# The leftover rows of w2: four loads of 32 rows made one load of 128 rows

## The chip, the cores and the metric

The kernel runs on one core of a Trainium2 chip. The metric is the device time of the whole program in microseconds, as the median of the runs of one kernel. The profile comes from one further execution, recorded by the hardware profiler. Its span, from the first to the last instruction, is a little shorter than the time of the same execution.

## The reference

The input x has 2048 rows of 640 elements in bf16. Two blocks are computed from it and mixed by a gate:

```python
x = A_x
g = _sigmoid((x * gate_w).sum(-1, keepdims=True))
a = _A_ref(x, A_wqkv, A_wo)                       # linear attention, 32 heads of 20
b = _B_ref(x, B_w1, B_w2, B_w3, B_w4)             # shift MLP, then an MLP with F = 1728
return g * a + (1 - g) * b
```

The part that the change touches is the middle of block B. There c is 160, and g0 to g3 are the four groups of c columns of h, shifted by 1, -1, 2 and -2 rows:

```python
h = _gelu(_layernorm(x, axis=-1) @ w1)
c = D // 4
...
hs = jnp.concatenate([g0, g1, g2, g3], axis=-1) @ w2
x1 = x + hs
h2 = _gelu(_layernorm(x1, axis=-1) @ w3) @ w4
return x1 + h2
```

## The kernel before, in words

A product over 640 columns is made in DC = 5 chunks of 128 rows of the weight, one chunk per matmul of an accumulation. The rows of x are worked on in 16 chunks of 128 (NCH) or in 4 tiles of 512 (NT).

The four groups of h that are shifted differently have 160 columns each (CG), which is not a multiple of 128. So the first 128 columns of group g make chunk g (g = 0 to 3), and the four leftovers of 32 columns share chunk 4: the leftover of group g lies in partitions 32g to 32g + 31. The activations in `hsT` and the rows of w2 in `w2_sb` are laid out in this way. `w2_sb[:, 4, :]` therefore holds rows 128 to 159, 288 to 319, 448 to 479 and 608 to 639 of w2.

All large loads are issued by SyncE (`sp`), in the order of the text: the first chunks of x and k's weights (some of these by ScalarE), x transposed by the DMA (L123), q's weights (L138), the rest of x (L120, called a second time), v's weights (L140), w1 (L141), six blocks of wo (L143), w2 (L144 to L148) and w3 (L149). w2's loads are one for the first two whole blocks (L144), then in a loop over g the strips of g = 0 and g = 1 (L148), the block of g = 2 (L147), its strip, the block of g = 3 and its strip. w4 is loaded much later (L602 to L604). A schedule written out by hand (`manual_schedule`) keeps the order of the text on every engine.

After w3, SyncE's queue holds the DMA transposes of the linear attention's matrix (L323, written from `gs`, which ScalarE evacuates at L321) and of the normalised rows of x (`lnx`, L311).

TensorE's order is: k (L187), q (L242), the sums over rows (L319), then for the first tile of rows the product with w1 (L353), the small products of the attention (L372, L257, L386), the product with w2 (`w2_unit`, L436, 5 chunks for each half of 320 columns), more of w1, then w3 (`w3_unit`, L486), interleaved with w2 for later tiles and with the attention's output (L467), and at last w4 (L525, L561). On GpSimd, L171 copies the leftover columns of w1 together once w1 has landed.

The few lines that matter here besides the diff:

```python
for hf in range(2):
    for fc in range(DC):
        nc.tensor.matmul(pt[:, hf, 0:HD], lhsT=hsT[:, fc, 2 + c * P:2 + (c + 1) * P],
                         rhs=w2_sb[:, fc, hf * HD:(hf + 1) * HD], start=(fc == 0), stop=(fc == DC - 1))
```

Of the kernel before, what the change touches and what calls it, by code (L numbers as in the profile page):

```python
# [16 lines left out]
def kernel(  # L17
# [14 lines left out]
    P = 128  # L32
# [12 lines left out]
    CG = D // 4  # L45
# [34 lines left out]
    w2_sb = const.tile([P, DC, D], BF16)  # L80
# [36 lines left out]
    sp, aq, gq = nc.sync, nc.scalar, nc.gpsimd  # L117
# [24 lines left out]
    for g in range(NG):  # L142
        sp.dma_start(wo_sb[:, g, :], A_wo[row0[g]:row0[g] + P, :])  # L143
    sp.dma_start(w2_sb[:, 0:2, :], B_w2[0:2 * CG, :].rearrange("(g p) f -> p g f", g=2)[0:P])  # L144
    for g in range(4):
        if g >= 2:
            sp.dma_start(w2_sb[:, g, :], B_w2[CG * g:CG * g + P, :])  # L147
        sp.dma_start(w2_sb[32 * g:32 * (g + 1), 4, :], B_w2[CG * g + P:CG * (g + 1), :])  # L148
    sp.dma_start(w3_sb[:], B_w3.rearrange("(c p) f -> p c f", p=P))  # L149


# [510 lines left out]
```

## Time and profile before

| What | Value |
|---|---|
| time, median of 3 runs | 263.35 us (263.07 to 265.75) |
| time of the profiled execution | 263.29 us |
| its span | 261.6 us |
| granted TensorE clock, mean | 0.998 |
| DMA packets, bytes | 57618, 28.28 MB |
| DVE, ACT, POOL busy | 141.3, 93.4, 28.0 us |
| first L436 (w2 is read) starts | 86.2 us |
| first L486 (w3 is read) starts | 102.4 us |

The times in a profile are microseconds from the start of the span. PE is TensorE, PEld its weight loads, DVE is VectorE, ACT is ScalarE, POOL is GpSimd; SPq is the queue of SyncE, which issues DMAs. `w_sb` stands for w1, w2, w3 and w4 alike, since the names are cut at the digits; the line tells them apart. The page's DMA row gives the mean busy share of the 16 DMA engines in 40 equal slices of the span, in tenths. The chain that ended last is followed back from the last instruction, at each step to what released it or to the instruction ahead of it on its engine.

### The profile page before, as it was taken

To read this page: it belongs to the slowest core of one execution; us is meant where nothing else is said; L and a number is where in the kernel's file an instruction comes from. 1 tells how busy PE (TensorE), PEld (TensorE's weight loads), DVE (VectorE), ACT (ScalarE), POOL (GpSimd) and SP (SyncE) were. 2 spreads that over 40 slices of the span, in tenths; PEclk is the share of its full clock that TensorE was granted. 3 is DMA by queue.
4 is the path that set the end of the run, shared out by engine and by line. 5 is a ranking of instruction groups with operands and counts; after the bars stand their busy time and mean duration, and the time that the engine had idled before them with its cause. 6 is when DMAs were issued, how large, how long until landed. Compare 5 with 4: busy or idle time off the path is not lost.

```text
span 261.6 us, 4116 instructions
## 1 busy us (share of the span) xinstructions
PE 255.6 (98%) x1601; PEld 151.4 (58%) x1625; DVE 141.3 (54%) x276; ACT 93.4 (36%) x144; POOL 28.0 (11%) x82
## 2 busy tenths in 40 slices
PE   7999999999999999999999999999999999999995
PEld 3777555688854644565464566455565555465553
DVE  2688778799947884866300398600287600125142
ACT  1555454321165446532343323342321443442100
POOL 3000040012220140131000131000122000000000
PEclk9999999999999999999999999999999999999999
DMA  7999996016675736997022124212123412211011
GB/s 200 201 185 370 364 287 267 0 28 123 123 103 77 213 71 139 173 315 95 7 43 40 20 53 95 75 23 60 20 53 70 102 20 43 65 34 64 0 50 53
DMA packets 57618, 28.28 MB, mean 108 GB/s; under 512 B 45566, under 2 KB 56830, under 8 KB 57598
## 3 DMA queue, kind: packets, MB, share of 16 engines
q1 hardware_dynamic: 57156, 27.52, 45.0%
q10 hardware_dynamic: 442, 0.49, 0.5%
q8 instruction: 13, 0.21, 0.3%
q14 instruction: 7, 0.06, 0.1%
HBM read 13.03 MB, written 3.60 MB: 64 GB/s over the span
## 4 chain that ended last, share of the span: by engine, by line
PE 96%; DMA 2%; issue 1%; SPq 0%; DVE 0%
PE pp L486 21%; PE pp L525 16%; PE pp L319 8%; PE pp L436 8%; PE pp L467 8%; PE pp L242 8%; PE pp L353 8%; PE pp L187 8%; PE pp L561 5%; DMA wk_sb<-in_A_wqkv_dram 2%; PE pp L496 1%; PE pp L517 1%; PE pp L386 1%; PE pp L372 1%; PE pp L257 0%
## 5 line engine op out<-in xcount | busy, mean ns | idle before, releaser
L486 PE MATMUL pp<-lnxT,w_sb 128*128 128x512 bf16 x249 | 59.8, 379 | 0.6
L488 ACT ACTIVATE h<-pp 128x1024 bf16<-128x1024 f32 (+1 forms) x28 | 26.9, 962 | 56.1 <-PE pp L486 56.1
L525 PE MATMUL pp<-h,w_sb 128*128 128x512 bf16 (+1 forms) x228 | 42.4, 343 | 0.3
L486 PEld LDWEIGHTS <-w_sb 128*128 128x128 bf16 x260 | 25.2, 98 | 26.9
L439 DVE TENSOR_TENSOR x<-pp,x_sb 128x640 f32<-128x640 f32 x16 | 13.1, 818 | 43.0 <-PE pp L436 42.9
L525 PEld LDWEIGHTS <-w_sb 128*128 128x128 bf16 x234 | 22.7, 98 | 19.5 <-issue 1.0
L179 ACT ACTIVATE e<-pp 128x640 bf16<-128x640 f32 (+1 forms) x26 | 21.5, 826 | 9.6 <-PE pp L242 9.6
L467 PE MATMUL pp<-m_sb,pqT 128*128 128x320 bf16 x160 | 24.3, 299 | 0.0
L473 DVE SCALAR_TENSOR_TENSOR x<-pp,gate,x 128x640 f32<-128x640 f32 x16 | 14.1, 883 | 18.3 <-PE pp L467 12.6
L436 PE MATMUL pp<-w_sb,hsT 128*128 128x320 bf16 x160 | 23.9, 299 | 0.0
L289 POOL TENSOR_SCALAR rstd<-mv 128x1 f32<-128x1 f32 (+1 forms) x20 | 7.7, 384 | 142.8 <-DVE mv L295 142.8
L187 PE MATMUL pp<-wk_sb,xT 128*128 128x320 bf16 (+1 forms) x160 | 22.5, 300 | 0.2
L319 PE MATMUL pp<-x_sb,pk 128*128 128x320 bf16 (+1 forms) x160 | 22.0, 300 | 0.0
L242 PE MATMUL pp<-xT,hsT 128*128 128x512 bf16 x98 | 21.6, 379 | 0.1
L319 PEld LDWEIGHTS <-pk 128*128 128x128 bf16 x160 | 18.8, 118 | 3.2
L436 PEld LDWEIGHTS <-hsT 128*128 128x128 bf16 x160 | 15.6, 98 | 8.0
L467 PEld LDWEIGHTS <-pqT 128*128 128x128 bf16 x160 | 15.7, 98 | 7.7
L538 DVE SCALAR_TENSOR_TENSOR oc<-pqT,omg,x 128x640 bf16<-128x640 bf16 x12 | 10.5, 877 | 16.8 <-DMA pqT<-hx 16.8
L187 PEld LDWEIGHTS <-xT 128*128 128x128 bf16 x160 | 15.5, 98 | 6.9 <-DVE xT L216 0.6
L353 PE MATMUL pp<-lnxT,w_sb 128*128 128x512 bf16 x77 | 17.9, 379 | 0.2
L242 PEld LDWEIGHTS <-hsT 128*128 128x128 bf16 x100 | 11.8, 118 | 9.7
L529 ACT CAST hx<-pp 128x512 bf16<-128x512 f32 x12 | 7.0, 585 | 22.5 <-PE pp L525 14.9
(80 smaller groups left out, 236.2 us busy)
## 6 DMA issues: line engine op xcount, KB each, us to landing
x_sb<-in_A_x_dram SPq DMA_DIRECT2D x1, 2240.0 KB
out_dram<-oc SPq DMA_DIRECT2D x14, 160.0 KB
w_sb<-in_B_w_dram SPq DMA_DIRECT2D x1, 2160.0 KB
w_sb<-in_B_w_dram SPq DMA_DIRECT2D x1, 2080.0 KB, 12.1
wo_sb<-in_A_wo_dram SPq DMA_DIRECT2D x6, 160.0 KB, 7.6
m_dram<-x SPq DMA_DIRECT2D x3, 320.0 KB, 2.8
hsT<-in_A_wqkv_dram SPq DMA_DIRECT2D x1, 800.0 KB, 5.7
m_sb<-in_A_wqkv_dram SPq DMA_DIRECT2D x1, 800.0 KB
```

Source lines behind the costliest of these rows:

```text
L179: nc.scalar.activation(ev, src, ACT.Exp)
L187: nc.tensor.matmul(pt[:, hf, 0:n], lhsT=xT[:, dc, c * P:(c + 1) * P], rhs=wk_sb[:, dc, hf * HD:hf * HD + n], start=(dc == first), stop=(dc ...
L242: nc.tensor.matmul(pt[:, t % 2, :], lhsT=wq_sb[:, dc, :].rearrange("p (m j) -> p j m", j=DC)[:, j], rhs=xT[:, dc, t * TS:(t + 1) * TS], st ...
L319: nc.tensor.matmul(pt[:, hf, 0:HD + hf], lhsT=w, rhs=x_sb[:, c, hf * HD:(hf + 1) * HD + hf], start=(c == 0), stop=(c == NCH - 1))
L353: nc.tensor.matmul(pt[:, i, :], lhsT=w, rhs=lnxT[t][:, dc, :], start=(dc == 0), stop=(dc == DC - 1))
L436: nc.tensor.matmul(pt[:, hf, 0:HD], lhsT=hsT[:, fc, 2 + c * P:2 + (c + 1) * P], rhs=w2_sb[:, fc, hf * HD:(hf + 1) * HD], start=(fc == 0), ...
L439: nc.vector.tensor_tensor(x1[:].rearrange("p (h e) -> p h e", h=2), pt[:, :, 0:HD], x_sb[:, c, 0:D].rearrange("p (h e) -> p h e", h=2), op ...
L467: nc.tensor.matmul(pt[:, hf, 0:HD], lhsT=pqT[:, j, c * P:(c + 1) * P], rhs=m_sb[:, j, hf * HD:(hf + 1) * HD], start=(j == 0), stop=(j == D ...
L473: nc.vector.scalar_tensor_tensor(x1, pt[:, :, 0:HD], gate[:, c:c + 1], x1, op0=ALU.mult, op1=ALU.add)
L486: nc.tensor.matmul(pt[:, k, :], lhsT=w3_sb[:, dc, fc * P:(fc + 1) * P], rhs=lnT[:, dc, :], start=(dc == 0), stop=(dc == DC - 1))
L488: nc.scalar.activation(h2[:, 2 * i * TS:(2 * i + n) * TS], pt[:].rearrange("p h e -> p (h e)")[:, 0:n * TS], ACT.Gelu_apprx_tanh)
L525: nc.tensor.matmul(dst, lhsT=w4_sb[:, fc, d * P:(d + 1) * P], rhs=st[t]["h2"][:, fc * TS + a:fc * TS + b], start=False, stop=(fc == FF - 1))
```

## The change

The loads of the whole blocks of g = 2 and g = 3 stay as they are. The four loads of 32 rows, one after each block, become one load behind the two blocks. Its destination is all 128 partitions of chunk 4; its source is a view of w2 as 4 groups of 160 rows, of which rows 128 to 159 of each are taken: 4 pieces of 32 rows that lie 160 rows apart. The bytes and where they go are the same. Nothing else differs.

```diff
     sp.dma_start(w2_sb[:, 0:2, :], B_w2[0:2 * CG, :].rearrange("(g p) f -> p g f", g=2)[0:P])
-    for g in range(4):
-        if g >= 2:
-            sp.dma_start(w2_sb[:, g, :], B_w2[CG * g:CG * g + P, :])
-        sp.dma_start(w2_sb[32 * g:32 * (g + 1), 4, :], B_w2[CG * g + P:CG * (g + 1), :])
+    for g in range(2, 4):
+        sp.dma_start(w2_sb[:, g, :], B_w2[CG * g:CG * g + P, :])
+    sp.dma_start(w2_sb[:, 4, :], B_w2.rearrange("(g p) f -> g p f", g=4)[:, P:CG, :])
     sp.dma_start(w3_sb[:], B_w3.rearrange("(c p) f -> p c f", p=P))
```

## The prediction

> **What bounds the kernel now.** I read the page's share of busy time first, then the chain that ended last, then the DMA row of the page, the SyncE queue's timeline around the edited loads, that queue's waits, and last the first readers of w2 and w3 on TensorE.
>
> ```profile
> span 261.6 us, 4116 instructions
> PE 255.6 (98%) x1601; PEld 151.4 (58%) x1625; DVE 141.3 (54%) x276; ACT 93.4 (36%) x144; POOL 28.0 (11%) x82
> DMA  7999996016675736997022124212123412211011
> PE 96%; DMA 2%; issue 1%; SPq 0%; DVE 0%
> ```
>
> TensorE is busy for 255.6 of 261.6 us, and 96% of the chain that ended last is TensorE. The DMA row has slices of 6.54 us: the engines are full from about 6 to 39 us, at 6 tenths in the next slice, and at 0 from 45.8 to 52.3 us. The edited loads run in the last full part, before that hole.
>
> ```profile
> 29.89 0.38 SPq L144 DMA_DIRECT2D w_sb<-in_B_w_dram  x1
> 32.29 0.81 SPq L148 DMA_DIRECT2D w_sb<-in_B_w_dram  x2
> 33.14 0.42 SPq L147 DMA_DIRECT2D w_sb<-in_B_w_dram  x1
> 33.61 0.43 SPq L148 DMA_DIRECT2D w_sb<-in_B_w_dram  x1
> 34.08 0.42 SPq L147 DMA_DIRECT2D w_sb<-in_B_w_dram  x1
> 34.55 0.43 SPq L148 DMA_DIRECT2D w_sb<-in_B_w_dram  x1
> 35.02 1.51 SPq L149 DMA_DIRECT2D w_sb<-in_B_w_dram  x1
> 54.42 1.21 SPq L323 DMA_TRANSPOSE wk_sb<-gs  x1
> ```
>
> Columns are start, duration, queue, line. The four strips are the L148 issues, the two whole blocks L147, and w3 follows at L149. After w3 the queue issues nothing until L323 at 54.42 us, 17.9 us after w3's issue ends.
>
> ```profile
> SPq L323 <- ACT gs L321: 17.1, 1, 17.1
> SPq L148 <- DMA w_sb<-in_B_w_dram: 2.0, 1, 2.0
> SPq L144 <- DMA m_sb<-in_A_wqkv_dram: 1.9, 1, 1.9
> SPq L323 <- DMA w_sb<-in_B_w_dram: 0.7, 1, 0.7
> ```
>
> These are waits of the queue up to 60 us. L144 waits for the load issued eight before it (wv at L140), the first L148 for the load eight before it (w1 at L141): a loading instruction waits until the eighth before it has landed. L323 waits 17.1 us for ScalarE's gs, so its time is set by compute, not by loads.
>
> ```profile
> 84.95 0.22 PE pp L353
> 85.17 0.05 issue
> 85.22 0.81 PE pp L353 x3
> 86.03 0.27 PE pp L386 x2
> 86.30 5.46 PE pp L436 x40
> ...
> 92.67 9.88 PE pp L353 x45
> 102.55 0.86 PE pp L486 x4
> ```
>
> This is the chain from 84 to 106 us. w2 is first read at L436, w3 at L486. Nothing stands between L386 and L436, or between L353 and L486: TensorE arrives there and goes on.
>
> **The change, part by part.**
>
> *Issues removed.* Four strip issues (0.81 + 0.43 + 0.43 = 1.67 us) become one of about 0.42 us, the duration of its L147 neighbours, so some 1.25 us of SyncE time goes. Six issues stand between 32.29 and 35.02 us now, three will: at the pitch of 0.47 us (34.08 to 34.55) w3 is issued at 32.29 + 3 x 0.47 = 33.70 us, 1.3 us earlier. On the path this is worth 0, because the work behind w3 on SyncE is L323, which waits for gs until 54.42 us.
>
> *Waits that move.* With three issues fewer, the eighth before shifts. g=2's block now meets w1's landing (32.29 us, as the first strip did); g=3's block waits for the first wo load, the new strip load for the second, w3 for the third. In the trace the second strip, the g=2 block and the third strip had those same predecessors and went out at about 32.7, 33.14 and 33.61 us without a wait. My issue times (32.76, 33.23, 33.70) lie just behind these, so no wait is added, at most a few tenths. L323's predecessor becomes the fourth wo load, landed long before. Price on the path: 0. GpSimd's w1x copies (L171) are released by w1's landing and keep their place.
>
> *The new transfer itself.* It carries the same 160 KB in 128 rows of 1,280 B. The stretch from 30 to 35 us moves 365 GB/s over 16 engines, 22.8 GB/s each, so a row costs 1,280 / 22.8 = 56 ns of one engine. Spread over 16 engines it is 8 rows each, as the four strips together are: 0.45 us, the same. How many engines the new shape reaches is shown nowhere in this trace: the source has an outer dimension of 4 blocks, each 32 rows long. I bound it. Best: 16 engines, no change. Worst by these rows: one engine, 128 rows, 7.2 us, that is 120 rows or 6.7 us more on that engine. With four engines it is 32 rows each, 24 more than now, 1.35 us. I take four, since the outer dimension is the only thing about the shape that differs from the whole blocks of 128 rows; for the time it does not matter which.
>
> *The rule against it.* The row here is the DMA share of 1.07 to 1.10 from 26 to 36 us: all engines full with loads of 128 and 32 rows, so none of these is seen confined. The Trainium skill, "DMA: Bandwidth & Descriptors", section "Rules for kernel authors", says that an outermost dimension of fewer than 16 confines a DMA to at most that many engines; by it the load sits on 4 engines. The same section says to coalesce small transfers into large ones, which speaks for the change. By the first rule the sum is 0 as well as by the second, because of the slack worked out next. No row of this trace decides between them.
>
> *What lies behind it.* w3's 2.2 MB now move from about 38 to 43.4 us (415 to 422 GB/s from 39 to 43 us, then 176, then 0 at 44). In a dip at 37 to 38 us (120 GB/s) the engines wait for w3's first data. Issued 1.3 us earlier, w3 fills part of the dip and follows w2's rows at about 37.2 us; 2.2 MB / 418 GB/s = 5.3 us put its end at 42.5 us, or 43.9 us with four engines, or some 49 us with one. w3 is first read at 102.4 us: slack 58 us, or 53 at worst. w2's strips are first read at 86.17 + 4 x 0.136 = 86.7 us (the fifth product of L436, 40 taking 5.46 us): slack about 49 us. The DMA transposes start at 54.42 us: even the worst end lies 5 us ahead of them.
>
> *TensorE.* The readers may have fewer loads to wait for (four instead of seven). The chain shows 0.05 us of issue at 85.17 us, before L386, and none at L436. What this can return is between 0 and 0.1 us; I take 0.
>
> *Sum.* 0 on the path; cover: the products of L242, L319 and L353, which keep TensorE busy through the whole stretch from 30 to 86 us (55.79 of 56 us). The profiled execution took 263.29 us, its span 261.6 plus 1.7 around it; the three runs have a median of 263.35, 0.06 above. Prediction: 263.3 us.
>
> **Rivals.**
>
> *1. Faster, because a load wait goes.* For a gain of 1% (2.6 us) TensorE would have to be idle where w2 or w3 is awaited. Its idle time is 0.05 us from 30 to 50, 0.16 from 50 to 86 and 0.11 from 86 to 105 us: 0.32 in all. If all of it went, the time would be 263.0 us. Against it: none of that idle time names a load. The 4.2 us idle behind 105 us stand between stages that read data of compute. I give 0.03 to a time below 263.0 us from this, and 0.01 of it to more than 1%.
>
> *2. Slower: the new shape moves in small pieces or over few engines, and the queue behind it is late.* This ends on the other side. For: the shape is new, and the queue holds w3 and all transposes behind it. Against: both sides of the load have whole rows of 640 contiguous elements, so nothing in the diff cuts a row. The point from which it decides: the strip must last over 11 us longer (w3 landed by 43.4, transposes from 54.42 us) to touch the transposes, about 15 us to make TensorE late (the first lnxT transposes are issued by 63.4, land within 4.0 and are read at 70.9 us, 3.5 us later). On one engine that needs 15 / 120 = 125 ns a row more than twice the 56 measured. If rows were cut into 256 B as the transposes are (1,212 packets in 24.8 engine-us from 50 to 60 us, 20 ns each), 640 pieces cost 13 engine-us, still hidden on one engine. If they were cut into single elements, 81,920 pieces at 20 ns are 1,640 engine-us, over 16 engines 102 us: w2 would land near 138 instead of 86.7 us, and the time would be about 263.3 + 51 = 314 us. Chance of a slower time by this: 0.04.
>
> *3. The change does what it says, but the load's bytes land unevenly and w3 comes 1 to 6 us later.* Hidden anyway: 263.3 us, the same forecast with another trace. It shares the forecast's chance.
>
> *4. A small shift of the rest.* A different instruction stream on SyncE can move transposes by tenths of a microsecond; one is seen tight: gs's fifth transpose is issued from 73.5 us and read at 76.34 us. It is issued 37 us behind w3 and waits for ScalarE (gs at 72.79 us), so I see no way for the edit to reach it. Price if it did: a few tenths, up to 264 us. Chance 0.04.
>
> **How the numbers follow.** Forecast with rival 3: 0.89; rival 1: 0.03; rival 4: 0.04; rival 2: 0.04. A measurement of this kernel can tell about 1% (2.6 us) from no change. Within 1% lie the forecast, most of rival 1 and rival 4: 0.94; faster 0.01; slower 0.05, rival 2 and a little of rival 4. The range: down to 262.6 us, that is rival 1's whole 0.32 us and the 0.28 us by which the lower runs differ (263.07 to 263.35); up to 264.4 us, rival 4 and somewhat under half of the 2.4 us by which one of the three runs stood above the median. Rival 2 lies outside, within the 2 in 10 left out.
>
> **What would show it.** Right: one strip issue instead of four, w3's issue near 33.7 us, w3's landing between 42 and 50 us, zero DMA traffic before 54 us, L323 still at about 54.4 and L436 at about 86.2 us with nothing between it and L386, TensorE busy for about 255.6 us. If the load reaches few engines, the DMA share drops under 1 while w2's last rows move and w3's landing spreads. Wrong: an idle TensorE released by a DMA at L436 or L486, DMA traffic that goes on past 54 us, many more DMA packets than 57,618, or a later lnxT at L353.

## The result and the profile after

The changed kernel takes 262.61 us in the median of 20 runs (262.12 to 263.07), the kernel before 263.26 us in the median of 20. The ratio is 0.9969, with a 95% interval of 0.9956 to 0.9981: 0.3% faster, small, but clear of no change. Its profiled execution took 262.68 us, with a span of 261.0 us (before: 263.29 and 261.6).

First the page of the changed kernel, the lines that answer to those of before: span, TensorE, DMA row, chain by engine.

```profile
span 261.0 us, 4113 instructions
PE 256.0 (98%) x1601; PEld 151.5 (58%) x1625; DVE 141.4 (54%) x276; ACT 93.5 (36%) x144; POOL 27.9 (11%) x82
DMA  7999996016684836994032123312123402211011
PE 98%; issue 1%; DVE 0%
```

TensorE is the bound as before. The hole in the DMA row is still there (the eighth slice, now 45.7 to 52.2 us). Next the SyncE queue's timeline around the edited loads; the line numbers are one lower than before from the edit on.

```profile
30.60 0.38 SPq L144 DMA_DIRECT2D w_sb<-in_B_w_dram  x1
32.89 0.80 SPq L146 DMA_DIRECT2D w_sb<-in_B_w_dram  x2
33.77 0.72 SPq L147 DMA_DIRECT2D w_sb<-in_B_w_dram  x1
34.54 0.43 SPq L148 DMA_DIRECT2D w_sb<-in_B_w_dram  x1
54.32 1.25 SPq L322 DMA_TRANSPOSE wk_sb<-gs  x1
```

The four strips are one issue (L147), w3 follows at 34.54 us, and the queue is again idle until L322. The DMA engines' load in two stretches shows what the new shape does (columns: stretch, length, busy time of PE, PEld, DVE, ACT and POOL with counts, granted clock, DMA share, GB/s). Before:

```profile
42.00:44.00 2.00, 2.00 (x11) 1.09 (x10) 1.49 (x3) 1.02 (x1) 0.00 (x0) 1.00 0.74 296
44.00:46.00 2.00, 2.00 (x11) 1.11 (x10) 1.58 (x2) 0.97 (x1) 0.00 (x0) 1.00 0.00 0
```

After:

```profile
42.00:44.00 2.00, 2.00 (x11) 1.09 (x10) 1.49 (x3) 1.02 (x1) 0.00 (x0) 1.00 0.57 221
44.00:46.00 2.00, 2.00 (x11) 1.05 (x9) 1.49 (x3) 1.02 (x1) 0.00 (x0) 1.00 0.07 28
```

The share falls to 0.57 at 42 to 44 us, and 0.07 is left after 44: most engines are done earlier, and a few work on, so the transfers have become uneven. The trace's records of landings say why. The strip load's counter gets one record at 34.9 us, just behind its issue, and then only 4, between 39.2 and 40.3 us, where the counters of the whole blocks get 16. Of w3's 16 increments, 11 come by 43.6 us and five from 44.6 to 45.5 us; before, the last came at 44.4 us. The Trainium skill, "DMA: Bandwidth & Descriptors", section "Rules for kernel authors", says that an outermost dimension of fewer than 16 confines a DMA to at most that many engines; with 4 engines for 4 groups the trace agrees. Nobody pays for it, as the chain from 84 to 106 us shows:

```profile
85.12 0.81 PE pp L352 x3
85.93 0.27 PE pp L385 x2
86.20 5.46 PE pp L435 x40
...
92.58 9.88 PE pp L352 x45
102.45 0.86 PE pp L485 x4
```

L435 (w2) and L485 (w3) follow without a gap, each 0.10 us earlier than before. That 0.10 us is older than the edit: q's first product starts at 27.45 us instead of 27.56, before any edited load is issued.

So the gain is elsewhere. The last VectorE instruction ends at 258.65 us (before 258.75), the span at 260.97 (before 261.58): of 0.61 us, 0.10 lie in front and 0.50 behind the last computation. There the cost is in the queue's own instructions, which a timeline of work leaves out: EVENT_SEMAPHORE, a wait for counters or for other engines, and DRAIN, which stands between such waits. The groups of the program's closing line show them. Before (columns: count, shortest/median/longest in ns, first and last start):

```profile
L657 SPq EVENT_SEMAPHORE  x7: 17/28/1116, 259.2 to 261.5; - x7
L657 SPq DRAIN  x3: 7/13/112, 260.6 to 261.3; - x3
```

After:

```profile
L656 SPq EVENT_SEMAPHORE  x7: 17/28/28, 259.1 to 260.9; - x7
L656 SPq DRAIN  x3: 7/7/13, 260.2 to 260.5; - x3
```

Before, one wait lasts 1,116 ns and one drain 112 ns; after, none lasts over 28 ns. The single records of SyncE, in order (number in its stream, counted from 0; then start, pause ahead of it and duration in us; the counters are those of DMA landings, numbered 0 to 7):

```
before (209 instructions)                      after (206 instructions)
198 258.774 0.179 0.332 last store, counter 2  195 258.680 0.170 0.333 last store, counter 7
199 259.152 0.046 1.116 wait counters 3, 2     196 259.059 0.046 0.028 wait counters 3, 2
200 260.309 0.041 0.028 wait counters 4, 1     197 259.128 0.041 0.027 wait counters 4, 1
201 260.376 0.039 0.028 wait counters 5, 0     198 259.368 0.213 0.028 wait counters 5, 0
202 260.440 0.036 0.028 wait 6, VectorE        199 259.594 0.198 0.028 wait 6, VectorE
203 260.530 0.062 0.028 wait 7, ScalarE        200 260.140 0.518 0.028 wait 7, ScalarE
204 260.600 0.042 0.013 first drain            201 260.205 0.037 0.013 first drain
205 260.660 0.047 0.007 drain                  202 260.275 0.057 0.007 drain
206 260.817 0.150 0.017 wait for the others    203 260.427 0.145 0.017 wait for the others
207 261.264 0.430 0.112 drain                  204 260.519 0.075 0.007 drain
208 261.522 0.146 0.017 wait for the others    205 260.906 0.380 0.017 wait for the others
```

By the traces' records every DMA of the program takes the next of eight counters, and the program ends with five waits that cover all eight in a fixed order. Before, the last store has counter 2, which is waited for first; once it has landed (260.245 us), the other four waits still have to be worked through, 0.355 us from the landing to the first drain. After, there are three DMAs fewer, the last store has counter 7, the waits ahead of it pass while it is under way, and 0.081 us are left. Besides, before there is a pause of 0.43 us ahead of instruction 207, which the changed kernel hasn't: from first drain to end 0.984 against 0.764 us. Not all of the pause shows in the time, since in the changed kernel the last wait for the others comes 0.38 us behind the drain, in the kernel before only 0.15 us.

### The profile page after: what moved, and what is told of

The parts are those of the page before. It is cut to its first block, busy times and chain, and to the rows that moved or that the text cites. A ratio compares the mean times of both kernels' runs of the same rounds, so it can differ in the third digit from the quotient of the medians.

```text
span 261.0 us, 4113 instructions
## 1 busy us (share of the span) xinstructions
PE 256.0 (98%) x1601; PEld 151.5 (58%) x1625; DVE 141.4 (54%) x276; ACT 93.5 (36%) x144; POOL 27.9 (11%) x82
## 4 chain that ended last, share of the span: by engine, by line
PE 98%; issue 1%; DVE 0%
PE pp L485 21%; PE pp L524 16%; PE pp L186 9%; PE pp L318 8%; PE pp L435 8%; PE pp L466 8%; PE pp L241 8%; PE pp L352 8%; PE pp L560 5%; PE pp L199 1%; PE pp L495 1%; PE pp L516 1%; PE pp L385 1%; PE pp L371 1%; PE pp L256 0%
## 5 line engine op out<-in xcount | busy, mean ns | idle before, releaser
L485 PE MATMUL pp<-lnxT,w_sb 128*128 128x512 bf16 x249 | 59.8, 379 | 0.6
L485 PEld LDWEIGHTS <-w_sb 128*128 128x128 bf16 x260 | 25.2, 98 | 26.9
L435 PE MATMUL pp<-w_sb,hsT 128*128 128x320 bf16 x160 | 23.9, 299 | 0.0
L435 PEld LDWEIGHTS <-hsT 128*128 128x128 bf16 x160 | 15.6, 98 | 8.0
```

The source lines that it names most:

```text
L485: nc.tensor.matmul(pt[:, k, :], lhsT=w3_sb[:, dc, fc * P:(fc + 1) * P], rhs=lnT[:, dc, :], start=(dc == 0), stop=(dc == DC - 1))
```

## The experiments

The count theory: what matters is the number of DMAs, through the last store's counter (0.27 us). For the other 0.22 us two theories stand against each other: by the place theory the pause stands at a fixed number of SyncE's instruction stream, by the counter theory of the pause it goes with the last store's counter. Against all of these stands the shape theory: the 128-row load itself, or the SyncE time that it saves, brings the gain. Each ratio is to runs of the kernel before that were timed together with the kernel in question; their medians are 263.26, 263.31 and 263.19 us in the three groups of runs.

### The two kernels again

> The kernel before once more, for the scatter of its profile. Count theory (what counts is the number of loads ahead of the last stores, because the eight completion counters are taken in turn and SyncE's last waits go through them in a fixed order): 263.3 us, and 1.3 us from the last landing to the end of the span again, of which about 0.36 us lie between the landing and SyncE's first drain. Scatter theory (the end differs from run to run by itself): another end, some 0.8 to 1.3 us. The start of q's first product (27.7 us) shows how much of the 0.1 us in front is scatter: the count theory has no say in it.

> The changed kernel once more. Count theory: 262.6 us, and again about 0.08 us from the last landing to SyncE's first drain; ratio to the kernel before about 0.9975. Scatter theory: the end lies anywhere between 0.8 and 1.3 us behind the last landing, and the ratio is 1 within its interval in the mean of such runs.

Measured: 263.19 us for the kernel before, ratio 1.000 (0.9991 to 1.001), and 262.68 us for the changed one, ratio 0.9974 (0.9963 to 0.9984). The end, from the last landing, is 1.332 and 0.856 us, in the first profiles 1.339 and 0.845: it does not scatter. q's first product starts at 27.76 and 27.77 us, so the start differs by 0.2 to 0.3 us between executions of one kernel, and the 0.10 us in front is scatter.

### The new strip load, with as many DMAs as before

```diff
-        sp.dma_start(w2_sb[:, g, :], B_w2[CG * g:CG * g + P, :])
+        for i in range(0, P, 32 if g == 2 else P):
+            n = 32 if g == 2 else P
+            sp.dma_start(w2_sb[i:i + n, g, :], B_w2[CG * g + i:CG * g + i + n, :])
```

> The one load of 128 rows for chunk 4 stays, but the whole block of g = 2 is loaded in four pieces of 32 rows, so that there are as many loads as in the kernel before and the last store falls on the same counter as there. Count theory: 263.3 us, the time of before, with about 0.36 us from the last landing to SyncE's first drain. Shape theory (the gain comes from the 128-row load of the strips itself, by earlier data or fewer engines in use): 262.6 us, the time of after, with the short end.

Measured: 263.52 us, ratio 1.0009 (0.9988 to 1.0031); 0.355 us from landing to first drain. The new load alone gains nothing.

### The old strips, with as many DMAs as after

```diff
-    for g in range(NG):
+    sp.dma_start(wo_sb[:, 0:NG:NG - 1, :], A_wo.rearrange("(c p) f -> p c f", p=P)[:, 0:DC:DC - 1, :])
+    for g in range(1, NG - 1):
         sp.dma_start(wo_sb[:, g, :], A_wo[row0[g]:row0[g] + P, :])
-    sp.dma_start(w2_sb[:, 0:2, :], B_w2[0:2 * CG, :].rearrange("(g p) f -> p g f", g=2)[0:P])
+    sp.dma_start(w2_sb[:, 0:4, :], B_w2.rearrange("(g p) f -> p g f", g=4)[0:P])
     for g in range(4):
-        if g >= 2:
-            sp.dma_start(w2_sb[:, g, :], B_w2[CG * g:CG * g + P, :])
...
```

> The four strip loads stay as before, but three other loads go: w2's four whole blocks are one load, and the first and last block of wo are one load. So there are as many loads as in the changed kernel, and the last store falls on its counter. Count theory: 262.6 us, with about 0.08 us from the last landing to SyncE's first drain. Shape theory: 263.3 us, since the strips are loaded as before.

Measured: 262.70 us, ratio 0.9978 (0.9969 to 0.9988); 0.081 us from landing to first drain. The strips are untouched and the gain is all there. With the run before it, the shape theory falls.

### More DMAs instead of fewer

```diff
     sp.dma_start(w3_sb[:], B_w3.rearrange("(c p) f -> p c f", p=P))
+    for i in range(5):
+        sp.dma_start(spare[:, i, :], B_w2[32 * i:32 * (i + 1), 0:16])
```

> The kernel before, four strip loads and all, with five spare loads of 1 KB from SyncE behind w3's load, into a tile that nothing reads (added work). Five more put the last store on the counter of the changed kernel. Count theory: 262.6 to 262.7 us, 0.08 us from the last landing to SyncE's first drain, although there are eight loads more than in the changed kernel and the strips are loaded as before; place theory: no pause at the last drain. Shape theory and a theory by which fewer issues gain time: 263.3 us or more.

> The kernel before with eight spare loads of 1 KB behind w3's load, issued by SyncE in its idle time, into a tile that nothing reads (added work; the output's computation is whole). Eight more is once round the eight counters: the last store falls on the same counter as in the kernel before, so from the last landing to SyncE's first drain there are 0.36 us again. Open is the other part of the end, SyncE's last drain, which came 0.43 us behind the instruction ahead of it in the kernel before (its instruction 207 of 209) and 0.08 us behind it in the changed kernel (206 instructions in all). Place theory (the pause stands at a fixed place of SyncE's stream, near its instruction 206, whatever stands there): with 217 instructions it falls earlier, into a wait, and the end is 0.22 us shorter: about 263.0 us. Counter theory (the pause belongs to the counter or the last store): 263.3 us and the pause again.

Measured with five: 262.86 us, ratio 0.9986 (0.9976 to 0.9997), the end 0.851 us, as in the changed kernel. The time is 0.2 us above what was expected, but there are eight DMAs more than in the changed kernel, and the end is the same. With eight: 263.08 us, ratio 0.9996 (0.9987 to 1.0004), which by itself does not tell the two expectations apart; the trace does. The wait for counter 2 stands first again (0.341 us to the first drain), and there is no pause at the last drain. It stands ahead of instruction 207, now the first wait (0.39 us), inside the time in which the last store is under way anyway.

### The counter and the place, apart

The counters are shared by both engines that issue DMAs, so spare loads from ScalarE move the last store's counter and leave SyncE's stream as it is.

```diff
         prs = [pair() for _ in range(3)]
         place(prs, {0: (0, 1), 2: (1, 2)})
+        for i in range(5):
+            aq.dma_start(spare[:, i, :], B_w2[32 * i:32 * (i + 1), 0:16])
```

(The lines stand ahead of the two quoted ones; in the second kernel there are three, added to the changed kernel.)

> The kernel before, with five spare loads of 1 KB issued by ScalarE ahead of the last w4 products, where ScalarE has nothing left to do (added work, into a tile that nothing reads). The counters are shared by both issuers, so the last store falls on the changed kernel's counter, while SyncE's stream keeps its 209 instructions. Count theory: 0.08 us from the last landing to SyncE's first drain. Place theory: the pause at the last drain stays, so 263.3 - 0.27 = 263.0 us. Counter theory of the pause: it goes, 262.7 us.

> The changed kernel, with three spare loads of 1 KB issued by ScalarE ahead of the last w4 products (added work, into a tile that nothing reads). The last store falls back on the counter of the kernel before, and SyncE's stream keeps the changed kernel's 206 instructions. Count theory: 0.36 us from the last landing to SyncE's first drain, 262.6 + 0.27 = 262.9 us. Place theory: no pause at the last drain. Counter theory of the pause: the pause again, 263.1 to 263.2 us.

The closing line's groups, first of the kernel before with five from ScalarE, then of the changed kernel with three:

```profile
L660 SPq EVENT_SEMAPHORE  x7: 17/28/28, 259.2 to 261.3; - x7
L660 SPq DRAIN  x3: 7/13/127, 260.4 to 261.0; - x3
```

```profile
L659 SPq EVENT_SEMAPHORE  x7: 17/28/1128, 259.1 to 261.2; - x7
L659 SPq DRAIN  x3: 7/7/13, 260.5 to 260.8; - x3
```

The long wait and the long drain go separately: the first kernel has only the drain, the second only the wait. Measured: 263.04 us, ratio 0.9992 (0.9984 to 1.0000), 0.086 us to the first drain and the pause in place; and 263.00 us, ratio 0.9989 (0.9968 to 1.001), 0.322 us and no pause. So the pause goes with the place and not with the counter. The two middle times lie where the sum of two terms puts them, though each ratio alone reaches 1.

### Two counters between

The same spare loads from SyncE, two and four of them.

> The kernel before with two spare loads of 1 KB from SyncE behind w3's load, into a tile that nothing reads (added work). The last store falls on the counter of SyncE's second wait of five, so three waits are left behind its landing instead of four. Count theory with steps of 0.07 us: 0.29 us from the last landing to SyncE's first drain (0.36 with four left, 0.08 with none). Place theory: of 211 instructions the one numbered 207 is now SyncE's second drain, so the pause stands there and costs about 0.35 us in the open. Together: no gain, 263.2 to 263.4 us. If neither held, the time would lie between before and after.

> The kernel before with four spare loads of 1 KB from SyncE behind w3's load, into a tile that nothing reads (added work). The last store falls on the counter of the fourth wait of five, one wait is left: 0.15 us from the last landing to SyncE's first drain by the count theory alone. Place theory: of 213 instructions number 207 is the fifth wait, the one behind the landing, so the pause of about 0.35 us stands there and that stretch is 0.5 us instead of 0.15; the last drain has no pause. Together about 263.1 to 263.3 us, although the counter alone would make it faster than before by 0.2 us.

Measured with two: 0.307 us to the first drain, and the pause of 0.39 us ahead of instruction 207, the second drain, as expected. The time is 263.70 us, ratio 1.0019 (1.0006 to 1.0032): slower than expected by 0.3 us, and slower than before. Of that the end explains 0.18 us (1.523 against 1.339), as much as the lower end of the ratio's interval asks for (0.16 us); no run places the rest, and the profiled execution, the fastest of the ten at 262.92 us, doesn't show it. With four: 0.520 us to the first drain, the pause of 0.39 us now being ahead of the fifth wait, and 263.28 us, ratio 0.9997 (0.9985 to 1.0008), as expected.

All kernels together, from the traces and the timed runs, in us:

| Kernel | SyncE instructions | last store's counter | landing to first drain | first drain to end | sum | median |
|---|---|---|---|---|---|---|
| before | 209 | 2 | 0.355 | 0.984 | 1.339 | 263.26 |
| new strip load, g = 2 split | 209 | 2 | 0.355 | 0.979 | 1.334 | 263.52 |
| before, 5 from ScalarE | 209 | 7 | 0.086 | 0.977 | 1.063 | 263.04 |
| before, 2 more | 211 | 4 | 0.307 | 1.216 | 1.523 | 263.70 |
| before, 4 more | 213 | 6 | 0.520 | 0.792 | 1.312 | 263.28 |
| before, 8 more | 217 | 2 | 0.341 | 0.770 | 1.111 | 263.08 |
| after, 3 from ScalarE | 206 | 2 | 0.322 | 0.768 | 1.090 | 263.00 |
| before, 5 more | 214 | 7 | 0.086 | 0.765 | 0.851 | 262.86 |
| old strips, 3 fewer elsewhere | 206 | 7 | 0.081 | 0.770 | 0.851 | 262.70 |
| after | 206 | 7 | 0.081 | 0.764 | 0.845 | 262.61 |

Median minus sum lies between 261.8 and 262.2 us for all ten kernels, while the sum goes from 0.85 to 1.52 us: the end accounts for the differences to within some 0.2 us either way. No kernel here ends sooner behind its last landing than the changed one, and nothing in the runs points to one that would.

## Why the prediction was right and wrong

*Bound, cover and transfer: right.* TensorE stays the bound, no wait for w2 or w3 appears, the transposes start when gs is ready. The load does reach four engines, as taken, w3 lands within the stretch given (42 to 50 us), and all of it costs nothing.

*Issue times: right in sign, off in size.* w3 was to be issued 1.41 us behind w1's landing (33.70 against 32.29). It came 1.65 us behind (34.54 against 32.89), because the strip's issue takes 0.72 us instead of 0.42 (0.73 us in the repeat). With the whole queue 0.6 to 0.7 us later in that execution, w3 went out only 0.5 us earlier than before, and landed at 45.5 us instead of the 43.9 given for four engines. The landing before had been read too early as well: 43.4 us from the GB/s, where the counter's last increment is at 44.4. The slack of over 50 us swallows this.

*The step that failed: the moved waits.* I had read from the queue's waits that a load waits for the eighth DMA before it, and followed the shift by three as far as L323. But the shift does not end there. Every later DMA takes another counter, the last stores too, and the closing waits go through the counters in an order that does not shift along. "Price on the path: 0" was right for the loads and wrong for the end of the program: 0.27 us, and with it the "0 on the path" of the sum.

*The step beside it: the idle time at the end.* Rival 1 put the 4.2 us of idle TensorE behind 105 us "between stages". Of these, 3.2 us lie behind its last product (258.4 to 261.6 us), where SyncE's last store, its landing and the closing waits are the path. The queue's waits of the kernel before over the whole span have a row for it, but the prediction shows them only up to 60 us:

```profile
SPq L657 <- DMA out_dram<-oc: 1.1, 1, 1.1
```

The second term in that stretch, the pause at instruction 207 (0.22 us), was not to be foreseen in size. But with three instructions fewer SyncE's stream ends ahead of number 207, and the prediction said only that a different stream may move transposes. Both terms together are 0.49 us that the sum had at 0.

*Rivals.* Rival 4, a small shift of the rest, had the kind of effect right and the place and the sign wrong; rival 1 had the sign, by a mechanism (a load wait that goes) that didn't take place; rival 2's lateness was there (w3 1.1 us later) and hidden, as argued against it. That 262.61 us still lies at the very edge of the range given, whose lower end is 262.6 us, is luck: that end was made of TensorE's idle time ahead of 105 us and of the scatter of the lower runs, and neither is what changed.

*What stays open.* The trace's end accounts for 0.49 us. The ratio of 0.9969 with its interval makes 0.50 to 1.16 us of 263.26 us, that of the repeat (0.9974) 0.42 to 0.97 us. The medians differ by 0.65 and 0.58 us. Some 0.1 to 0.2 us may lie elsewhere, and the profiles, whose starts differ by more, can't show it.

## What to carry to other kernels

When an edit changes how many DMAs there are, follow the consequences to the last instruction: which counter does the last store get, and how many closing waits are left behind its landing? Differences of 0.1 to 0.2% (0.27 us for the counter, 0.49 us with the pause, of 263 us) can have this cause alone, so check an edit that should do nothing with a second kernel that has the same DMA count without the edit. And read the stretch behind the last computation as a stage of its own, in the records of the queue that ends the program.

## What the runs showed of the hardware

SyncE pauses at a fixed place of its own instruction stream. Ahead of number 207 there are 0.38 to 0.43 us in every trace that has so many instructions, whatever the instruction is: the first, fourth or fifth closing wait, the second or the last drain. Where it meets a wait for a landing it costs nothing. In the open it costs 0.2 us ahead of the last drain (0.98 against 0.77 us from the first drain to the end) and 0.45 us ahead of the second (1.22 against 0.77). Number 79, 128 earlier, has 0.44 us or more ahead of it in all twelve traces. The page's instruction queues move 13 packets of 0.21 MB and 7 of 0.06 MB in all, some 16 and 8 KB each, so a refill of the instruction memory is a likely cause. The packets' times speak for it: in all twelve traces one of the 8 KB packets starts 0.0 to 2.1 us behind the start of number 79, whether that comes at 86.7 or at 95.4 us, and in the eight traces with a number 207 one starts 0.6 to 0.9 us behind it, in some of them after the span's end. That the refill makes the engine pause is still inferred; no run here shows it. The Trainium skill, "Runtime: NRT & Kernel Launch", section "Instruction fetch mechanics", says that crossing from one block of instructions to the next costs little and is mostly hidden, with blocks of 256 instructions; if this is that crossing, the runs differ in the distance (128) and in the cost where nothing hides it.
